# A retention, gated-FFN and four-expert kernel: low parts of the down weights by accumulating transfers, a product's operand straight from its bank, and seven products in the last unit too

## The chip, the cores and the metric

One Trainium2 chip, one of its cores. The metric is device time in microseconds of one execution; lower is better. All arithmetic on the matrix engine is fp32 split into parts: a matrix is written as high part plus low part (both in the short fp32r form), and a product of two matrices is three matrix multiplications, high by high, high by low, low by high.

## The reference

Three layers follow one another on 1536 tokens of width 512:

```python
for t in range(S):                       # B2, H8, S768, D64
    state = gamma[None, :, None, None] * state + np.einsum('bhd,bhe->bhde', k[:, :, t], v[:, :, t])
    y[:, :, t] = scale * np.einsum('bhd,bhde->bhe', q[:, :, t], state)
...
xn = x / rms * rms_g                     # DFF 1536
return (silu * val @ w_out)              # silu = g * sigmoid(g), g = xn @ w_gate, val = xn @ w_val
...
for e in range(E):                       # E 4, F 1024
    h = np.maximum(x @ w1[e], 0.0)
    out += p[:, e:e + 1] * (h @ w2[e])   # p: domain_probs over their sum
```

The change lies in the last layer, the four experts.

## The kernel before, in words

The experts' hidden columns (4 x 1024) are cut into N2 = 16 units u of 256 columns; the tokens into two halves g = 0 and 1 of 768. For each (u, g) there are an up product (512 by 256 columns of w1) and a down product (256 by 512 of w2), whose result is scaled by the expert's probability and added into `oacc[g]`.

**Up.** `winograd()` (L570) computes a 2-by-2 block product from seven products p1 to p7 instead of eight, each of 12 matmuls of 384 columns (L586). Sums of the weights' blocks (`sums`, L364) and of the tokens' blocks stand in for the blocks. PSUM banks are copied to SBUF where a product is needed twice (`kept`, L595, on ScalarE).

**Down.** `expert_out` (L1436) is plain: 6 token tiles, for each 6 matmuls of 512 columns (L1457 to L1459). `mixed_out` (L1368) takes seven products n instead, each of 9 matmuls of 256 columns (L1420), in the order n = 1, 4, 6, 5, 7, 3, 2; its weights are the two plain tiles of w2 and four differences of their quarters (`down`, made by `down_sums`, L514), its operands n the hidden blocks or sums of them (`h`, L1328). It is used for g = 0 in the units of `MIXED`, 1 to 14. Its results are added to `oacc` by VectorE (L1397): at product 7 two adds from the banks `cross`.

**Operands of the seven.** `mixed_use` (L1315) makes the operands of `mixed_out`: ReLU on ScalarE (L1339, L1346), sums by L1328, then for each operand n the high part `hs` by a ScalarE cast (L1320) and the low part `hs` by a subtraction on GpSimd or VectorE (L1322). Operand 6 is the sum made from operand 5, and that from operand 7's sum; operand 3 is made from operand 6's sum. In `expert_use`, for the units' second half, VectorE adds the kept bank (L1299), ScalarE makes the high part (L1302), VectorE the low one (L1306).

**Order on TensorE.** Within a unit: p1, p2 of (u, 0); three tiles of `expert_out` of (u-1, 1); p5, p6, p3, p7; the other three tiles; p4; then, one by one in turn, the products of (u, 1) and of `mixed_out` of (u, 0): p1, n1, p2, n4, p5, n6, p6, n5, p3, n7, p7, n3, p4, n2. One such period takes 30.6 us.

**Weights.** `piece_tasks` (L304) loads a piece of w1 or w2 (SyncE), makes its high part with ScalarE (L401) and its low part with a subtraction, `widelo` and `plainlo` (L406). `down_sums` does the same with its four differences: high part by L521, low part `downlo` by L525.

**Who does what, when.** `Pace` (L32) is a planner that runs while the program is written. A piece of work that may go to GpSimd or VectorE is added as "PV" with a level and a size, and a table of costs decides the engine and the place in its queue. Every engine then works its queue strictly in order; nothing is decided on the chip. A change of the tasks or of a cost thus moves the queues of GpSimd, VectorE and ScalarE in all later units.

Of the kernel before, what the change touches and what calls it, by code (L numbers as in the profile page):

```python
# [7 lines left out]
F32 = mybir.dt.float32  # L8
# [3 lines left out]
AF = mybir.ActivationFunctionType  # L12
ALU = mybir.AluOpType
PSUM = bass.MemoryType.PSUM

P = 128
# [146 lines left out]
def tile_retention_gated_experts(  # L163
# [27 lines left out]
    nc = tc.nc  # L191
# [8 lines left out]
    D = DM // H  # L200
# [11 lines left out]
    N2 = E * UPE  # L212
    HD = DM // 2
    MORE_HS = 2
    MIXED = set(range(1, N2 - 1))
    SEVEN = {(u, g) for u in (1,2,3,4,) for g in (1,)}
    STAGED = 3
    BIG = 3
# [85 lines left out]
    def piece_tasks(n):  # L304
# [98 lines left out]
        def low_part(eng, half):  # L403
            hi, lo = wt[key] if is_wide(key) else wt[key + (j,)]
            for t, at in parts(half):
                eng.tensor_tensor(out=at(lo), in0=t, in1=at(hi).bitcast(F32), op=ALU.subtract)  # L406

        def then(engines, size, run, *deps, gate=None, port=True):
            return pace.add(1 if key in (("g", 0), ("v", 0), ("2", 0)) else 2, engines, size, run, deps, gate, port)

# [12 lines left out]
        for half in range(2 if is_wide(key) else 1):  # L423
            size = 384 if is_wide(key) and half == 0 else NC
            last = source
            if half == 1:
                for i in range(4):
                    before = (sums_done[-2:-1] if double else sums_done[-1:]) if i == 0 else []
                    last = then("PV", P, lambda eng, i=i: sums(eng, i), last, *before)
            hi = then(  # L430
                "A", size, lambda eng, half=half: high_part(eng, half), last, *highs[-1:], gate=lambda: has_slot(key)
            )
            highs.append(hi)
            lows.append(then("PV", size, lambda eng, half=half: low_part(eng, half), hi))
        if is_wide(key):
            sums_done.append(lows[-1])
        if double:
# [58 lines left out]
    def down_sums(u, then):  # L496
# [19 lines left out]
        def high(eng, half):  # L516
# [3 lines left out]
                ]  # L520
            eng.copy(out=wt[key][0][:, 2 * half:2 * half + 2].rearrange("p n d -> p (n d)"), in_=got["t"][half])  # L521

        def low(eng, half):
            hi, lo = (w[:, 2 * half:2 * half + 2].rearrange("p n d -> p (n d)") for w in wt[key])
            eng.tensor_tensor(out=lo, in0=got["t"][half], in1=hi.bitcast(F32), op=ALU.subtract)  # L525

        gate = lambda: "T" in pools and (
            all(("S", x) in used for x, g in SEVEN) if u == min(MIXED) else u - 1 in sums_used
# [8 lines left out]
        free1 += steps[1:]  # L537
        for half in range(2):
            hi = then("A", 512, lambda eng, half=half: high(eng, half), steps[2 * half + 1], gate=gate)
            lows.append(then("PV", 512, lambda eng, half=half: low(eng, half), hi))  # L540
        tops_free.append(lows)
        ready[key] = lows

# [227 lines left out]
    def seven_out(u, g, hs):  # L771
# [7 lines left out]
        for n, half, blk in order:  # L779
# [4 lines left out]
            for j in range(KH):  # L784
# [19 lines left out]
                    [pace.done(pace.now)], port=False,  # L804
                ))
                open_chain.append(at[onto][j][-1])
            if n == 3 and g == max(x for y, x in SEVEN if y == u):
                w_used(("S", u))
            if n == 4 and g == G - 1:
                w_used(("o", u))  # L810
# [382 lines left out]
    def pair():  # L1193
        (hi, a), (lo, b) = any_tile(), any_tile()
        return hi, lo, (a, b)
# [119 lines left out]
    def mixed_use(hs):  # L1315
        h, done, read = {}, {}, {}

        def operand(n, t, dep):
# [5 lines left out]
            hs[n] = hi, lo, low, tags  # L1324
            return high, low

        def sub(out, x, y, op, *deps):
            return pace.add(0, "PV", TB, lambda eng: eng.tensor_tensor(out=out, in0=x, in1=y, op=op), deps)  # L1328

        def use(f, blk, a, b):  # L1330
# [15 lines left out]
                    0, "A", TB, lambda eng: eng.activation(out=t, in_=t, func=AF.Relu), [pace.done(end)]  # L1346
                )
            if at == (0, 0):
                read[1] = operand(1, t, done[at])
            elif at == (0, 1):  # L1350
                done[7] = sub(h[7], h[0, 0], t, ALU.subtract, done[0, 0], done[at])
                operand(7, h[7], done[7])
            elif at == (1, 1):
                operand(4, t, done[at])
                done[5] = sub(h[0, 1], h[0, 1], t, ALU.add, done[7], done[at])
                done[6] = sub(h[0, 0], h[0, 1], h[0, 0], ALU.subtract, done[5], *read[1])
                operand(5, h[0, 1], done[5])
                operand(6, h[0, 0], done[6])
            else:
                two = operand(2, t, done[at])  # L1360
                done[3] = sub(t, t, h[0, 0], ALU.subtract, done[6], *two)
                operand(3, t, done[3])
            return end
        return use

    open_sums = []

    def mixed_out(u, g, hs):  # L1368
        e = u // UPE
# [20 lines left out]
        def add(c, blk, cols, ps):  # L1390
            t = blk * CPB + c
            acc = oacc[g][:, t, cols]
            pe = p_sb[:, g * 2 * CPB + t, e:e + 1]
            if ps.shape[1] != acc.shape[1]:
                acc = acc.rearrange("p (h d) -> p h d", h=2)
                ps = ps.unsqueeze(1).to_broadcast([P, 2, HD])
            run = lambda eng: eng.scalar_tensor_tensor(out=acc, in0=ps, scalar=pe, in1=acc, op0=ALU.mult, op1=ALU.add)  # L1397
            return pace.add(1, "V", 512 if cols == every else HD + 100, run, [pace.done(pace.now)], port=False)

        plan = (  # L1400
            (1, plain_part(0, low_half), cross, lambda c: c != 1, (0, low_half, cross)),
# [7 lines left out]
        for n, moving, where, opens, result in plan:  # L1409
# [18 lines left out]
            if result:  # L1428
                blk, cols, ps = result
                for c in range(CPB):  # L1430
                    at[c].append(add(c, blk, cols, ps[c]))
                    open_sums.append(at[c][-1])
            pace.fill(3 * CPB * 0.12)
            yield

    def expert_out(u, g, hs):  # L1436
        e = u // UPE
        if u == N2 - 1:
            pace.need(*open_sums)
        w = weights(("2", u))  # L1440
        if u == 0:
            oacc.append(accp.tile([P, 2 * CPB, DM], F32, tag=f"acc{g}", name=f"oacc{g}"))
# [190 lines left out]
```

## Time and profile before

| what | value |
|---|---|
| median of 3 runs | 845.06 us (845.0 to 845.2) |
| the profiled execution, its own time | 845.45 us |
| its span, first to last instruction | 843.6 us |
| granted TensorE clock, mean | 0.998 |
| busy: TensorE, VectorE, ScalarE, GpSimd | 99%, 63%, 54%, 75% of the span |

The profile is of one execution. Around the span lie 1.85 us of its time. In the rows, PE is the matmul side of TensorE and PEld its weight loads, which overlap; DVE is VectorE, ACT ScalarE, POOL GpSimd, SP SyncE. "Idle before" an instruction, with the name of what ended it, is how a wait is read. The seven-product part of the experts begins at about 362 us, and TensorE's work ends at 839.8 us.

### The profile page before, as it was taken

The numbers are of one execution on the slowest core, as the hardware profiler recorded it, in microseconds if no ns is written. First come the engines' busy times: TensorE is split into PE (matmuls) and PEld (weight loads), VectorE is DVE, ScalarE is ACT, GpSimd is POOL, SyncE is SP. The second block draws the span as 40 slices with busy tenths as digits, with TensorE's granted clock in tenths as the row PEclk, the third lists the DMA queues.
The fourth block names the chain that finished last, engine by engine and source line by source line (L and its number), as shares of the span: only waits on it lengthen the run. The fifth ranks groups of instructions, "written<-read, shape, count | busy, mean of one in ns | idle before, by whom it ended". The sixth has DMA issues, their size and how long they took to land.

```text
span 843.6 us, 13967 instructions
## 1 busy us (share of the span) xinstructions
PE 831.1 (99%) x5143; PEld 791.8 (94%) x5143; DVE 534.6 (63%) x959; ACT 457.6 (54%) x1023; POOL 634.7 (75%) x753
## 2 busy tenths in 40 slices
PE   8989999999999999999999999999999999999998
PEld 7889999999999999889999999999999999999987
DVE  3886665877778657834565566466466556556654
ACT  4878886666665456665544544545444454454421
POOL 3457886597979676869888988988988988987500
PEclk9999999999999999999999999999999999999999
DMA  7951231232121111011011011010011011101003
GB/s 258 310 187 51 76 126 59 68 84 68 54 97 38 51 38 38 26 38 36 28 38 38 26 46 31 26 51 26 26 51 38 25 38 38 39 26 38 1 13 137
DMA packets 29232, 52.37 MB, mean 62 GB/s; under 512 B 3988, under 2 KB 12724, under 8 KB 29164
## 3 DMA queue, kind: packets, MB, share of 16 engines
q1 hardware_dynamic: 28880, 51.24, 19.3%
q8 instruction: 40, 0.66, 0.3%
q10 hardware_dynamic: 284, 0.24, 0.1%
q14 instruction: 28, 0.23, 0.1%
HBM read 48.33 MB, written 3.15 MB: 61 GB/s over the span
## 4 chain that ended last, share of the span: by engine, by line
PE 79%; DVE 7%; POOL 6%; ACT 6%; issue 2%; DMA 1%; DVEq 0%; POOLq 0%; ACTq 0%
PE bank L586 39%; PE bank L1420 7%; PE bank L1458 6%; PE bank L1459 6%; PE bank L1457 6%; PE cross L1420 5%; PE bank L797 2%; POOL widelo L406 1%; PE bank L930 1%; PE bank L1267 1%; PE bank L1268 1%; PE bank L1266 1%; PE bank L912 1%; POOL sums L364 1%; DVE sums L364 1%
## 5 line engine op out<-in xcount | busy, mean ns | idle before, releaser
L595 ACT COPY kept<-bank 128x384 f32<-128x384 f32 x150 | 71.9, 480 | 117.3 <-PE bank L586 108.0
L1397 DVE SCALAR_TENSOR_TENSOR oacc<-cross,p_sb,oacc 128x256 f32<-128x256 f32 (+1 forms) x126 | 65.6, 565 | 64.2 <-PE cross L1420 64.2
L1465 DVE SCALAR_TENSOR_TENSOR oacc<-bank,p_sb,oacc 128x512 f32<-128x512 f32 (+1 forms) x97 | 72.3, 745 | 51.9 <-PE bank L1459 51.8
L1322 POOL TENSOR_TENSOR hs<-h,hs 128x384 fp32r<-128x384 f32 x97 | 97.5, 1025 | 0.8 <-ACT hs L1320 0.8
L586 PE MATMUL bank<-x2Thi,widehi 128*128 128x384 f32 x256 | 87.7, 343 | 0.7 <-DVE kept L1299 0.7
L586 PE MATMUL bank<-x2Thi,widelo 128*128 128x384 f32 x256 | 86.2, 337 | 0.0
L586 PE MATMUL bank<-x2Tlo,widehi 128*128 128x384 f32 x256 | 85.9, 336 | 0.0
L1459 PE MATMUL bank<-plainhi,hs 128*128 128x512 f32 (+1 forms) x218 | 85.1, 390 | 0.0
L1458 PE MATMUL bank<-plainlo,hs 128*128 128x512 f32 (+1 forms) x218 | 85.0, 390 | 0.0
L1457 PE MATMUL bank<-plainhi,hs 128*128 128x512 f32 (+1 forms) x218 | 84.3, 387 | 0.0
L1302 ACT ACTIVATE hs<-kept 128x384 fp32r<-128x384 f32 x54 | 28.4, 526 | 86.9 <-DVE kept L1299 86.8
L406 POOL TENSOR_TENSOR widelo<-sums,widehi 128x512 fp32r<-128x512 f32 x49 | 63.9, 1303 | 6.5 <-ACT widehi L401 5.8
L525 POOL TENSOR_TENSOR downlo<-down,downhi 128x512 fp32r<-128x512 f32 x28 | 36.3, 1296 | 37.8 <-ACT downhi L521 37.8
L586 PE MATMUL bank<-xThi,widehi 128*128 128x384 f32 x192 | 64.5, 336 | 0.1
L586 PE MATMUL bank<-xThi,widelo 128*128 128x384 f32 x192 | 64.2, 334 | 0.0
L586 PE MATMUL bank<-xTlo,widehi 128*128 128x384 f32 x192 | 64.2, 334 | 0.0
L1397 DVE SCALAR_TENSOR_TENSOR oacc<-bank,p_sb,oacc 128x512 f32<-128x512 f32 x84 | 59.1, 744 | 6.4 <-PE bank L1420 6.3
L1328 POOL TENSOR_TENSOR h<-h 128x384 f32<-128x384 f32 x55 | 56.1, 1019 | 4.2 <-ACT h L1346 2.2
L1320 ACT CAST hs<-h 128x384 fp32r<-128x384 f32 x98 | 48.9, 513 | 16.5 <-POOL h L1328 15.2
L586 PEld LDWEIGHTS bank<-x2Thi,widehi 128*128 128x128 f32 x256 | 48.2, 188 | 4.4 <-DVE kept L1299 3.0
L1343 DVE TENSOR_TENSOR h<-bank,kept 128x384 f32<-128x384 f32 x42 | 23.3, 554 | 45.1 <-PE bank L586 44.5
L406 POOL TENSOR_TENSOR widelo<-wst,widehi 128x256 fp32r<-128x256 f32 x64 | 37.1, 601 | 17.3 <-ACT widehi L401 17.3
(240 smaller groups left out, 2689.7 us busy)
## 6 DMA issues: line engine op xcount, KB each, us to landing
wst<-in_moe_w_dram SPq DMA_DIRECT2D x64, 256.0 KB, 2.8
qk<-in_qk_dram SPq DMA_DIRECT2D x12, 512.0 KB, 5.7
wst<-in_moe_w_gate_dram SPq DMA_DIRECT2D x12, 512.0 KB, 3.8
wst<-in_moe_w_val_dram SPq DMA_DIRECT2D x12, 512.0 KB, 3.8
wst<-in_moe_w_out_dram SPq DMA_DIRECT2D x12, 512.0 KB, 3.9
vk<-in_vk_dram SPq DMA_DIRECT2D x10, 512.0 KB, 5.4
out_dram<-oacc SPq DMA_DIRECT2D x11, 256.0 KB, 2.0
vk<-in_vk_dram SPq DMA_DIRECT2D x2, 256.0 KB, 4.1
```

What stands on the lines that cost most here:

```text
L406: eng.tensor_tensor(out=at(lo), in0=t, in1=at(hi).bitcast(F32), op=ALU.subtract)
L586: nc.tensor.matmul(out=ps, lhsT=lhs, rhs=rhs, start=(first and j == i == 0), stop=(j == KH - 1 and i == 2), skip_group_check=not first,)
L595: nc.scalar.copy(out=t, in_=ps)
L1320: high = pace.add(0, "A", TB, lambda eng: eng.copy(out=hi, in_=t), [dep])
L1322: 0, "PV", TB, lambda eng: eng.tensor_tensor(out=lo, in0=t, in1=hi.bitcast(F32), op=ALU.subtract), [high]
L1328: return pace.add(0, "PV", TB, lambda eng: eng.tensor_tensor(out=out, in0=x, in1=y, op=op), deps)
L1397: run = lambda eng: eng.scalar_tensor_tensor(out=acc, in0=ps, scalar=pe, in1=acc, op0=ALU.mult, op1=ALU.add)
L1420: nc.tensor.matmul(out=where[c], lhsT=lhs[:, cols], rhs=rhs, start=bool(i == 0 and opens and opens(c)), stop=(i == 2), skip_group_check=True,)
L1457: nc.tensor.matmul(out=ps, lhsT=hi[:, c], rhs=whi[:, cols], start=(f == 0), stop=False)
L1458: nc.tensor.matmul(out=ps, lhsT=hi[:, c], rhs=wlo[:, cols], start=False, stop=False)
L1459: nc.tensor.matmul(out=ps, lhsT=lo[:, c], rhs=whi[:, cols], start=False, stop=(f == NF - 1))
L1465: nc.vector.scalar_tensor_tensor(out=acc, in0=ps, scalar=pe, in1=acc, op0=ALU.mult, op1=ALU.add)
```

## The change

`MIXED` now holds unit 15 as well, so that its g = 0 half also goes through `mixed_out`; its output tiles leave by tasks (`leaving`) after products 7 and 2. For the w2 weights of every unit in `MIXED`, the low parts are no longer subtracted: ScalarE writes the negative high part into the low tile (it copies the source with scale -1), and a transfer issued by GpSimd adds the source onto it, from DRAM for the two plain tiles, from SBUF for the two tiles of differences (four transfers of 256 KB a unit). Operand 2 takes its high and low part straight from the PSUM bank (`direct`). The planner's level of VectorE's adds from `mixed_out` goes from 1 to 0, and the weights of the SEVEN units are given back at n = 7 instead of n = 3.

```diff
--- before.py
+++ after.py
@@ -212,7 +212,7 @@
     N2 = E * UPE
     HD = DM // 2
     MORE_HS = 2
-    MIXED = set(range(1, N2 - 1))
+    MIXED = set(range(1, N2))
     SEVEN = {(u, g) for u in (1,2,3,4,) for g in (1,)}
     STAGED = 3
     BIG = 3
@@ -405,6 +405,16 @@
             for t, at in parts(half):
                 eng.tensor_tensor(out=at(lo), in0=t, in1=at(hi).bitcast(F32), op=ALU.subtract)
 
+        def negative(eng):
+            (t, at), = parts(0)
+            eng.activation(out=at(wt[key + (j,)][1]), in_=t, func=AF.Copy, scale=-1.0)
+
+        def remainder(eng):
+            (t, at), = parts(0)
+            eng.dma_start(
+                out=at(wt[key + (j,)][1]), in_=src.rearrange("p h f -> p (h f)"), accum_op=ALU.add
+            )
+
         def then(engines, size, run, *deps, gate=None, port=True):
             return pace.add(1 if key in (("g", 0), ("v", 0), ("2", 0)) else 2, engines, size, run, deps, gate, port)
 
@@ -431,7 +441,11 @@
                 "A", size, lambda eng, half=half: high_part(eng, half), last, *highs[-1:], gate=lambda: has_slot(key)
             )
             highs.append(hi)
-            lows.append(then("PV", size, lambda eng, half=half: low_part(eng, half), hi))
+            if key[0] == "2" and key[1] in MIXED:
+                minus = then("A", size, negative, hi)
+                lows.append(then("P", 200, remainder, minus, port=False))
+            else:
+                lows.append(then("PV", size, lambda eng, half=half: low_part(eng, half), hi))
         if is_wide(key):
             sums_done.append(lows[-1])
         if double:
@@ -520,9 +534,15 @@
                 ]
             eng.copy(out=wt[key][0][:, 2 * half:2 * half + 2].rearrange("p n d -> p (n d)"), in_=got["t"][half])
 
+        def negative(eng, half):
+            eng.activation(
+                out=wt[key][1][:, 2 * half:2 * half + 2].rearrange("p n d -> p (n d)"), in_=got["t"][half],
+                func=AF.Copy, scale=-1.0,
+            )
+
         def low(eng, half):
-            hi, lo = (w[:, 2 * half:2 * half + 2].rearrange("p n d -> p (n d)") for w in wt[key])
-            eng.tensor_tensor(out=lo, in0=got["t"][half], in1=hi.bitcast(F32), op=ALU.subtract)
+            lo = wt[key][1][:, 2 * half:2 * half + 2].rearrange("p n d -> p (n d)")
+            eng.dma_start(out=lo, in_=got["t"][half], accum_op=ALU.add)
 
         gate = lambda: "T" in pools and (
             all(("S", x) in used for x, g in SEVEN) if u == min(MIXED) else u - 1 in sums_used
@@ -537,7 +557,8 @@
         free1 += steps[1:]
         for half in range(2):
             hi = then("A", 512, lambda eng, half=half: high(eng, half), steps[2 * half + 1], gate=gate)
-            lows.append(then("PV", 512, lambda eng, half=half: low(eng, half), hi))
+            hi = then("A", 512, lambda eng, half=half: negative(eng, half), hi)
+            lows.append(then("P", 200, lambda eng, half=half: low(eng, half), hi, port=False))
         tops_free.append(lows)
         ready[key] = lows
 
@@ -804,7 +825,7 @@
                     [pace.done(pace.now)], port=False,
                 ))
                 open_chain.append(at[onto][j][-1])
-            if n == 3 and g == max(x for y, x in SEVEN if y == u):
+            if n == 7 and g == max(x for y, x in SEVEN if y == u):
                 w_used(("S", u))
             if n == 4 and g == G - 1:
                 w_used(("o", u))
@@ -1324,6 +1345,15 @@
             hs[n] = hi, lo, low, tags
             return high, low
 
+        def direct(n, ps):
+            hi, lo, tags = pair()
+            nc.scalar.activation(out=hi, in_=ps, func=AF.Relu)
+            end = pace.did("A", TB)
+            nc.vector.scalar_tensor_tensor(
+                out=lo, in0=ps, scalar=0.0, in1=hi.bitcast(F32), op0=ALU.max, op1=ALU.subtract
+            )
+            hs[n] = hi, lo, pace.done(pace.did("V", TB, end)), tags
+
         def sub(out, x, y, op, *deps):
             return pace.add(0, "PV", TB, lambda eng: eng.tensor_tensor(out=out, in0=x, in1=y, op=op), deps)
 
@@ -1346,7 +1376,11 @@
                     0, "A", TB, lambda eng: eng.activation(out=t, in_=t, func=AF.Relu), [pace.done(end)]
                 )
             if at == (0, 0):
-                read[1] = operand(1, t, done[at])
+                if b is None:
+                    direct(1, a)
+                    read[1] = ()
+                else:
+                    read[1] = operand(1, t, done[at])
             elif at == (0, 1):
                 done[7] = sub(h[7], h[0, 0], t, ALU.subtract, done[0, 0], done[at])
                 operand(7, h[7], done[7])
@@ -1357,13 +1391,13 @@
                 operand(5, h[0, 1], done[5])
                 operand(6, h[0, 0], done[6])
             else:
-                two = operand(2, t, done[at])
-                done[3] = sub(t, t, h[0, 0], ALU.subtract, done[6], *two)
+                direct(2, a)
+                done[3] = sub(t, t, h[0, 0], ALU.subtract, done[6], done[at])
                 operand(3, t, done[3])
             return end
         return use
 
-    open_sums = []
+    open_sums, leaving = [], []
 
     def mixed_out(u, g, hs):
         e = u // UPE
@@ -1395,7 +1429,7 @@
                 acc = acc.rearrange("p (h d) -> p h d", h=2)
                 ps = ps.unsqueeze(1).to_broadcast([P, 2, HD])
             run = lambda eng: eng.scalar_tensor_tensor(out=acc, in0=ps, scalar=pe, in1=acc, op0=ALU.mult, op1=ALU.add)
-            return pace.add(1, "V", 512 if cols == every else HD + 100, run, [pace.done(pace.now)], port=False)
+            return pace.add(0, "V", 512 if cols == every else HD + 100, run, [pace.done(pace.now)], port=False)
 
         plan = (
             (1, plain_part(0, low_half), cross, lambda c: c != 1, (0, low_half, cross)),
@@ -1430,13 +1464,17 @@
                 for c in range(CPB):
                     at[c].append(add(c, blk, cols, ps[c]))
                     open_sums.append(at[c][-1])
+                    if u == N2 - 1 and n in (7, 2):
+                        t = blk * CPB + c
+                        acc, to = oacc[g][:, t, :], out[(g * 2 * CPB + t) * P:(g * 2 * CPB + t + 1) * P, :]
+                        leaving.append(pace.add(1, "D", 0, lambda eng, acc=acc, to=to: eng.dma_start(out=to, in_=acc), [at[c][-1]]))
             pace.fill(3 * CPB * 0.12)
             yield
 
     def expert_out(u, g, hs):
         e = u // UPE
         if u == N2 - 1:
-            pace.need(*open_sums)
+            pace.need(*open_sums, *leaving)
         w = weights(("2", u))
         if u == 0:
             oacc.append(accp.tile([P, 2 * CPB, DM], F32, tag=f"acc{g}", name=f"oacc{g}"))
```

`direct(1, a)` never runs: at (0, 0) the second argument is always given in these units.

In numbers of instructions: TensorE keeps its order but for the last unit, where 36 matmuls of 512 columns become 63 of 256. GpSimd goes from 758 to 626 instructions, 60 of them the new transfers; it gives up 58 low parts of w2, 24 low parts of operands and about 110 sums and low parts of w1, most of these two kinds to VectorE, which goes from 961 to 1115. ScalarE goes from 1018 to 1087 (60 negatives and 14 ReLUs from the bank more). SyncE's queue is the same. Up to 362 us all queues are the same.

The queue of GpSimd (POOL) in a middle unit, from the last differences of the down weights to operand 3. First before; `hs_7683`, `7673`, `7685`, `7687`, `7738`, `7740` are the low parts of operands 4, 7, 5, 6, 2, 3:

```order
L514 TENSOR_TENSOR down_7661<-wst_7636,wst_7533 128x256
L514 TENSOR_TENSOR down_7661<-wst_7636,down_7660 128x256
L1328 TENSOR_TENSOR h_7669<-h_7598,h_7670 128x384
L1322 TENSOR_TENSOR hs_7683<-h_7669,hs_7682 128x384
L1328 TENSOR_TENSOR h_7670<-h_7670,h_7669 128x384
L1328 TENSOR_TENSOR h_7598<-h_7670,h_7598 128x384
L1322 TENSOR_TENSOR hs_7673<-h_7669,hs_7672 128x384
L1322 TENSOR_TENSOR hs_7685<-h_7670,hs_7684 128x384
L1322 TENSOR_TENSOR hs_7687<-h_7598,hs_7686 128x384
L1322 TENSOR_TENSOR hs_7738<-h_7735,hs_7737 128x384
L1328 TENSOR_TENSOR h_7735<-h_7735,h_7598 128x384
L406 TENSOR_TENSOR widelo1_7585<-sums_7626,widehi1_7584 128x4x128
```

And the same stretch with the change, in units 2 to 13 alike; `hs_8424`, `8411`, `8426`, `8428` are the low parts of operands 4, 7, 5, 6:

```order
L406 TENSOR_TENSOR widelo1_8337<-sums_8366,widehi1_8336 128x4x128
L528 TENSOR_TENSOR down_8413<-wst_8250 128x256
L528 TENSOR_TENSOR down_8413<-wst_8388,down_8413 128x256
L1358 TENSOR_TENSOR h_8407<-h_8330,h_8408 128x384
L528 TENSOR_TENSOR down_8414<-wst_8388,wst_8250 128x256
L1343 TENSOR_TENSOR hs_8424<-h_8407,hs_8423 128x384
L364 TENSOR_TENSOR sums_8455<-wst_8439 128x128
L1343 TENSOR_TENSOR hs_8411<-h_8407,hs_8410 128x384
L1358 TENSOR_TENSOR h_8408<-h_8408,h_8407 128x384
L1358 TENSOR_TENSOR h_8330<-h_8408,h_8330 128x384
L1358 TENSOR_TENSOR h_8476<-h_8476,h_8330 128x384
L1343 TENSOR_TENSOR hs_8426<-h_8408,hs_8425 128x384
```

The row that follows is `hs_8428`, operand 6. The low part `widelo` of w1's sums (128x4x128) and the sum of operand 3 (`h_8476`), which stood behind operand 6's low part, now stand ahead of it, with one `sums`; the low part of operand 2 is gone from this queue.

The same queue in unit 14 with the change, where the transfers of the last unit's plain low parts come into it:

```order
L1343 TENSOR_TENSOR hs_9124<-h_9107,hs_9123 128x384
L1343 TENSOR_TENSOR hs_9111<-h_9107,hs_9110 128x384
L528 TENSOR_TENSOR down_9114<-wst_9088,down_9113 128x256
L414 DMA plainlo0_9163<-in_moe2_w2_dram 128x512
L1358 TENSOR_TENSOR h_9108<-h_9108,h_9107 128x384
L1358 TENSOR_TENSOR h_9030<-h_9108,h_9030 128x384
L414 DMA plainlo1_9194<-in_moe2_w2_dram 128x512
L1358 TENSOR_TENSOR h_9173<-h_9173,h_9030 128x384
L1343 TENSOR_TENSOR hs_9128<-h_9030,hs_9127 128x384
L1343 TENSOR_TENSOR hs_9180<-h_9173,hs_9179 128x384
```

Here two transfers stand between operand 7's low part (`hs_9111`) and operand 6's (`hs_9128`); operand 5's low part is VectorE's.

The queue of VectorE (DVE) around product 7's adds in a middle unit, before; `kept_8147` is the sum that frees the bank of p4:

```order
L1299 TENSOR_TENSOR kept_8170<-bank_8140,kept_8170 128x384
L1397 SCALAR_TENSOR_TENSOR oacc0_4346<-bank_8104,p_sb_81,oacc0_4346 128x512
L1397 SCALAR_TENSOR_TENSOR oacc0_4346<-cross_8100,p_sb_81,oacc0_4346 128x512 x2
L1299 TENSOR_TENSOR kept_8147<-bank_8088,kept_8147 128x384
L1306 SCALAR_TENSOR_TENSOR hs_8126<-kept_8096,hs_8125 128x384
L1306 SCALAR_TENSOR_TENSOR hs_8194<-kept_8170,hs_8193 128x384
```

and with the change, where `kept_8899` is that sum:

```order
L1320 TENSOR_TENSOR kept_8923<-bank_8892,kept_8923 128x384
L1431 SCALAR_TENSOR_TENSOR oacc0_4344<-bank_8852,p_sb_81,oacc0_4344 128x512
L1327 SCALAR_TENSOR_TENSOR hs_8948<-kept_8923,hs_8947 128x384
L1431 SCALAR_TENSOR_TENSOR oacc0_4344<-cross_8848,p_sb_81,oacc0_4344 128x512
L1320 TENSOR_TENSOR kept_8899<-bank_8836,kept_8899 128x384
L1431 SCALAR_TENSOR_TENSOR oacc0_4344<-cross_8848,p_sb_81,oacc0_4344 128x512
```

One low part and one add from `cross` stand between the last add from a bank and the sum, where two adds stood; the low part of p2's block (`hs_8875<-kept_8844`, not shown) also moves to the middle of the unit.

## Rows read from the trace of the kernel before

**Rows 1.** The page, part 1: busy time, share of the span, instructions, by engine.

```profile
PE 831.1 (99%) x5143; PEld 791.8 (94%) x5143; DVE 534.6 (63%) x959; ACT 457.6 (54%) x1023; POOL 634.7 (75%) x753
```

**Rows 2.** Windows, one period: length, busy PE, PEld, DVE, ACT, POOL; clock, DMA share, GB/s.

```profile
739.43:770.02 30.59, 30.59 (x185) 28.93 (x184) 18.18 (x32) 14.37 (x32) 26.89 (x33) 1.00 0.12 35
```

**Rows 3.** Waits: engine, line <- releaser: us in all, times, longest.

```profile
PEld bank L586 <- DVE kept L1299: 3.0, 13, 1.0
```

**Rows 4.** Timeline of POOL, same period: start, us, engine, line, operation, [idle before].

```profile
743.96 1.29 POOL L406 TENSOR_TENSOR widelo<-sums,widehi 128x512 fp32r<-128x512 f32 x1
745.21 1.02 POOL L1322 TENSOR_TENSOR hs<-h,hs 128x384 fp32r<-128x384 f32 x1
...
748.55 0.46 POOL L364 TENSOR_TENSOR sums<-wst,sums 128x128 f32<-128x128 f32 x1
748.97 0.74 POOL L514 TENSOR_TENSOR down<-wst 128x256 f32<-128x256 f32 x1
749.78 0.74 POOL L514 TENSOR_TENSOR down<-wst,down 128x256 f32<-128x256 f32 x1
750.48 0.74 POOL L514 TENSOR_TENSOR down<-wst 128x256 f32<-128x256 f32 x1
...
751.89 1.01 POOL L1328 TENSOR_TENSOR h<-h 128x384 f32<-128x384 f32 x1
752.86 1.02 POOL L1322 TENSOR_TENSOR hs<-h,hs 128x384 fp32r<-128x384 f32 x1
753.83 2.12 POOL L1328 TENSOR_TENSOR h<-h 128x384 f32<-128x384 f32 x2
755.90 3.94 POOL L1322 TENSOR_TENSOR hs<-h,hs 128x384 fp32r<-128x384 f32 x4
```

**Rows 5.** Timeline of ACT, same period.

```profile
747.94 0.48 ACT L595 COPY kept<-bank 128x384 f32<-128x384 f32 x1 [0.56 <-PE bank L586]
...
750.08 0.61 ACT L401 CAST widehi<-sums 128x512 fp32r<-128x512 f32 x1
```

**Rows 6.** Timeline of TensorE, same period: product n = 6 and what follows it.

```profile
760.28 0.28 PE L1420 MATMUL cross<-downhi,hs 128*128 128x256 f32 x1
...
760.40 0.30 PEld L1420 LDWEIGHTS cross<-downhi,hs 128*128 128x128 f32 x2
...
761.34 0.34 PE L586 MATMUL bank<-x2Thi,widehi 128*128 128x384 f32 x1
```

**Rows 7.** Timeline of all engines, same period: from product 7's adds to p4.

```profile
765.89 1.40 DVE L1397 SCALAR_TENSOR_TENSOR oacc<-cross,p_sb,oacc 128x512 f32<-128x512 f32 x2
...
767.21 0.54 DVE L1299 TENSOR_TENSOR kept<-bank,kept 128x384 f32<-128x384 f32 x1
...
767.56 0.28 PE L1420 MATMUL bank<-plainhi,hs 128*128 128x256 f32 x1
767.67 1.02 DVE L1306 SCALAR_TENSOR_TENSOR hs<-kept,hs 128x384 fp32r<-128x384 f32 x2
767.81 0.19 PEld L586 LDWEIGHTS bank<-x2Thi,widehi 128*128 128x128 f32 x1 [0.17 <-DVE kept L1299]
```

**Rows 8.** The costliest groups: POOL's low parts of operands, all 97.

```profile
L1322 POOL TENSOR_TENSOR hs<-h,hs 128x384 fp32r<-128x384 f32 x97 | 97.5, 1025 | 0.8 <-ACT hs L1320 0.8
```

**Rows 9.** DMA issues: what, queue, count, KB each, median us to landing; timeline of SP.

```profile
wst<-in_moe_w_dram SPq DMA_DIRECT2D x64, 256.0 KB, 2.8
...
773.36 0.34 SPq L316 DMA_DIRECT2D wst<-in_moe_w_dram  x1
```

**Rows 10.** Timeline of PE, last unit: three tiles of the plain down product of g = 0.

```profile
802.58 0.39 PE L1457 MATMUL bank<-plainhi,hs 128*128 128x512 f32 x1
...
806.71 0.33 PE L586 MATMUL bank<-x2Thi,widehi 128*128 128x384 f32 x1
```

**Rows 11.** Timeline of DVE and POOL, the period after: two low parts at once.

```profile
782.67 0.57 DVE L1322 TENSOR_TENSOR hs<-h,hs 128x384 fp32r<-128x384 f32 x1
...
782.79 1.33 POOL L1322 TENSOR_TENSOR hs<-h,hs 128x384 fp32r<-128x384 f32 x1
```

## The prediction

> **What bounds the kernel now.** I read the shares of the page first [rows 1]: TensorE is busy 99% of the span, the next engine, GpSimd, 75%. So the sum of TensorE's work is the time, and a change pays only by taking matmuls away or by ending a wait of TensorE; it costs whatever new wait it makes. Then the window of one period of the expert part [rows 2]: of 30.59 us TensorE works 30.59, while GpSimd works 26.89 and VectorE 18.18. The reader should see that GpSimd is close to full yet makes nobody wait. Taking 58 subtractions from GpSimd relieves an engine that is not waited for. Third, the list of waits: in the expert part TensorE has one wait that repeats, 13 times for 3.0 us in all, for VectorE's sum that frees the bank of p4 [rows 3]. That is what there is to win. Last the timelines, to see how much slack the operands of the seven down products have, since the order on TensorE stays the same but the queues of its feeders do not.
>
> **Low parts by transfers.** Removed from GpSimd: 58 subtractions. They stood beside matmuls, and nobody waited. Added on ScalarE: 60 negatives of about 0.6 us (the cast of as many elements takes 0.61 [rows 5]), 2.4 us per period on an engine that works 14.4 of 30.6 [rows 2]; nothing, so long as they stand behind the urgent ones, and if that cover goes ScalarE's kept copy comes up to 0.6 late. Added on GpSimd: 60 issues, of price D. The trace of before has no transfer issued by GpSimd. Bounds: 0.34 us, an issue on SyncE's queue, and 2.8 us, a 256 KB transfer from issue to landing [rows 9]. I take 1.0, near their geometric middle, since the issue is nearer to what an engine's queue is held for than the landing. The Trainium skill, "DMA: Bandwidth & Descriptors", Specifications, gives about 1 us to the first byte of a transfer issued by GpSimd; by that estimate the sum would be the same. In the units 2 to 13 the four issues stand where GpSimd has nothing urgent behind them: two after operand 3's low part, two at the unit's start. Landing is used 15 us later or more. The removed subtractions were 1.3 us each, so GpSimd has room. Cost there 0. The transfers' traffic, 1 MB a period on queues that are 12% busy, costs 0 too.
>
> **The moved chain: operand 6.** This is the main term. Before, GpSimd went from the differences through h7, operand 4, h5, h6 and operands 7, 5, 6; the third of the four low parts that start at 755.90 is operand 6's [rows 4], so it ended at 755.90 + 2 x 0.97 + 1.02 = 758.86. TensorE loads the weights of the first matmul that reads it at 760.40, just after product 6 begins at 760.28 [rows 6]: 1.5 us of slack. With the change `widelo` stands ahead of this chain, and it cannot start before ScalarE has cast the sums' high part, which now stands behind ScalarE's copy of p6. That copy starts at 747.94, released by TensorE, and takes 0.48; the cast takes 0.61 [rows 5]: 749.03. From there, start to start by the rows of [rows 4]: widelo 1.25 (743.96 to 745.21), two differences 0.81 + 0.70, h7 0.97, a difference 0.70, operand 4 0.97, a `sums` 0.42, operand 7 0.97, h5 and h6 2.07, the sum of operand 3 1.04 (half of that pair), operand 5 0.97, operand 6 1.02 to its end. Sum 11.89, so it ends at 760.92, and with 0.06 until the reader starts (in [rows 7] the sum ends at 767.75, the load it releases starts at 767.81) at 760.98. Needed at 760.40: TensorE stands 0.58 us. The chain is anchored to TensorE within each unit, so the wait does not melt away in later units: 12 units alike, 2 to 13, 12 x 0.58 = **+7.0**. The ends: 0.3 us (the steps of the chain at their fastest, 0.02 each lower) and 0.9 (a step or two beside a VectorE subtraction), 3.6 to 10.8. Behind the waiting matmuls stand all of TensorE's; nothing overtakes. Operands 5, 7 and 3 are needed later than they come.
>
> In unit 1 the chain is shorter and in unit 15 VectorE has part of it: 0. In unit 14 two issues of transfers come between operand 7 and operand 6, while operand 5 is VectorE's, there is no `sums`, and one difference more stands ahead: 11.89 - 0.97 - 0.42 + 0.70 = 11.20, and 2 D. From 749.03 to 760.40, less the 0.06, there are 11.31: about 2 D - 0.1 late, **+1.9** at D = 1.0, 0.6 to 5.5 between the bounds.
>
> **Product 7's adds and p4.** Before, two adds from `cross`, 1.40 us as a pair, precede the sum that frees p4's bank; the sum starts at 767.21, ends at 767.75, and TensorE's last matmul of n = 3 started at 767.56, with the next one due 0.12 later at 767.68. It started at 767.81 [rows 7]: 0.13 lost. With the change one add (0.66, half the start-to-start of the pair) and one low part (about 0.47 start to start, from the 1.02 for two) stand ahead: 0.19 earlier, so the wait goes. 12 x 0.13 = **-1.6** (0 to -3.0, all of [rows 3]). What is late next there is nothing: the bank's readers are done.
>
> **Operand 2 from the bank.** Its high part becomes a ReLU in place of a cast, on ScalarE both; its low part goes from GpSimd to VectorE, which is idle a third of the period; operand 2 is read last of all: 0. The weights freed at n = 7 instead of n = 3, and the level of the adds: they move queue places that are counted above, 0 by themselves.
>
> **The last unit.** 18 matmuls of 512 take 802.58 to 806.71 = 4.13 us [rows 10], so 36 take 8.26. Nine matmuls of a seven-product take 760.28 to 761.34 = 1.06 [rows 6], seven of them 7.42. **-0.8**. The adds behind it are 128x256 and 128x512 pieces on VectorE, beside matmuls of p1 to p7 of the other half; the output transfers leave before the end. The end itself, the last plain tile with its add and transfer, is the same.
>
> **Sum**, on the profiled execution: 845.45 + 7.0 + 1.9 - 1.6 - 0.8 = 851.95. It stood 0.4 over the median of the runs shown: **851.6**.
>
> **Rivals.**
> *A, the forecast*: 851.6, on its own 847 to 856.
> *B, the two low parts collide.* VectorE's low part of p2's block moves to the middle of the unit, beside GpSimd's operands 5 and 6, if ScalarE's high part for it comes early. When such a pair ran at once before, GpSimd's subtraction took 1.33 us instead of 1.025 [rows 11, 8]. That would be 0.31 a unit more: 12 x 0.31 = 3.7, so 855.3. Against: I find VectorE's to be ready some 0.2 us after GpSimd's last has begun. The Trainium skill, "SBUF — State Buffer", Who interferes with whom, says that a VectorE instruction with two SBUF inputs and a GpSimd one that reads SBUF lock each other out whole, the second waiting for the first. The trace agrees in kind but not in full: GpSimd started 0.12 after VectorE's 0.57 us and lost 0.31 instead of 0.45.
> *C, on the other side: operand 6 comes in time.* The wait vanishes if the chain is 0.58 us, 5% of its 11.9, shorter, or its start that much earlier (a cast that ScalarE does before its copy, say); from 11.3 us downward nothing is lost. Then 845.45 + 0.6 to 1.9 - 1.6 - 0.8 = 843.65 to 844.95, less 0.4: 843.3 to 844.6. For it: the chain is put together from single rows. Against: the 97 low parts of operands on GpSimd have a mean of 1025 ns [rows 8], so the steps hardly vary.
> *D, the issue is dear.* With D at 2.8 unit 14 loses 5.5 instead of 1.9, 855.2; and GpSimd's differences, pushed later, then run beside VectorE's low parts, up to the 3.7 of B more: 858.9. Against: an issue need not last until the landing.
> *E, the last unit's saving is not there*, as its operands come late to TensorE: 0.8 more, inside A's range.
>
> **How the numbers follow.** A 0.60 with E, B 0.15, D 0.08, C 0.17. What a measurement of this kernel can tell from no change is about 0.2%, 1.7 us: below 843.4 is faster, above 846.8 slower. C lies about 843.4 and above, 0.09 faster (with a shorter issue or more won at p4) and 0.08 same; 0.03 of A ends within 0.2%. Faster 0.09, same 0.11, slower 0.80. The range leaves out the lower half of C and the upper part of D: 844.0 to 858.0; the slower cases alone have 847 to 858.
>
> **What would show it.** Right: among the waits of TensorE a new group at the matmuls of `cross` (n = 6) released by GpSimd's low part `hs`, 12 or 13 times, about 0.6 us each, a period of 31.0 to 31.1 us, and one longer in unit 14. The 13 waits on VectorE's kept sum are gone or down to a few. GpSimd's busy time falls by over 100 us with an idle stretch ahead of `widelo` in each period: a relieved engine, and a later one. The last unit's g = 0 shows 63 matmuls of 256. B shows as low parts on GpSimd of 1.3 us where operand 6's stands, D as a wait in unit 14 of over 3 us. Wrong would be a period of 30.4 to 30.6 with no wait at n = 6 (then C), or a wait of TensorE on a weight's low part, whose transfer would have landed late.

## The result and the profile after

| | median | lowest to highest |
|---|---|---|
| before, beside it | 845.03 us | 844.69 to 845.20 |
| the change | 851.43 us | 851.29 to 852.02 |
| a second run of both: before | 844.31 us | 843.98 to 844.57 |
| the change | 851.32 us | 851.02 to 851.62 |

Ratio 1.0076 (95% interval 1.0058 to 1.0095), in the second run 1.0082 (1.0067 to 1.0098): slower by some 0.8%. The forecast was 851.6 us, with a wait of 0.58 us at product 6 in twelve units. The first part of the profile's page, the busy time of each engine, against [rows 1]:

```profile
PE 831.5 (98%) x5170; PEld 792.5 (93%) x5170; DVE 598.7 (70%) x1113; ACT 490.7 (58%) x1092; POOL 531.7 (63%) x621
```

GpSimd was relieved of 103 us, and the kernel got slower. The list of TensorE's waits, against [rows 3]:

```profile
PEld cross L1454 <- POOL hs L1343: 8.3, 13, 1.5
...
PEld bank L607 <- DVE kept L1320: 1.0, 1, 1.0
```

The 12 waits of 0.17 us before p4 are gone (a single one of 1.0, ahead of 360 us, is in both kernels); 13 new ones stand at product 6. GpSimd's timeline in the period of unit 13, which answers to [rows 4]:

```profile
753.69 1.29 POOL L406 TENSOR_TENSOR widelo<-sums,widehi 128x512 fp32r<-128x512 f32 x1 [5.23 <-ACT widehi L401]
754.95 0.74 POOL L528 TENSOR_TENSOR down<-wst 128x256 f32<-128x256 f32 x1
755.76 0.75 POOL L528 TENSOR_TENSOR down<-wst,down 128x256 f32<-128x256 f32 x1
756.46 1.01 POOL L1358 TENSOR_TENSOR h<-h 128x384 f32<-128x384 f32 x1
757.43 0.74 POOL L528 TENSOR_TENSOR down<-wst 128x256 f32<-128x256 f32 x1
758.13 1.02 POOL L1343 TENSOR_TENSOR hs<-h,hs 128x384 fp32r<-128x384 f32 x1
759.11 0.46 POOL L364 TENSOR_TENSOR sums<-wst 128x128 f32<-128x128 f32 x1
759.53 1.01 POOL L1343 TENSOR_TENSOR hs<-h,hs 128x384 fp32r<-128x384 f32 x1
760.51 3.19 POOL L1358 TENSOR_TENSOR h<-h 128x384 f32<-128x384 f32 x3
763.66 1.98 POOL L1343 TENSOR_TENSOR hs<-h,hs 128x384 fp32r<-128x384 f32 x2
```

Read it from the bracket: GpSimd stands idle 5.23 us, its queue held by `widelo`, which waits for ScalarE's cast. Then it works without a gap to the end of operand 6's low part, 763.66 + 1.98 = 765.64: 11.95 us for what this text calls the chain. TensorE and VectorE at that place, against [rows 6]:

```profile
764.71 1.35 DVE L1327 SCALAR_TENSOR_TENSOR hs<-kept,hs 128x384 fp32r<-128x384 f32 x1 [1.05 <-ACT hs L1323]
...
764.94 0.28 PE L1454 MATMUL cross<-downhi,hs 128*128 128x256 f32 x1
...
765.70 0.30 PEld L1454 LDWEIGHTS cross<-downhi,hs 128*128 128x128 f32 x2 [0.56 <-POOL hs L1343]
...
766.63 0.34 PE L607 MATMUL bank<-x2Thi,widehi 128*128 128x384 f32 x1
```

Product 6 runs from 764.94 to 766.63, 1.69 us where it took 1.06: TensorE loses 0.63, of which the row of the load shows 0.56. Unit 14's load at 797.70 has 1.50, its product 6 takes 2.62. The period, against [rows 2], now 31.07:

```profile
743.86:774.93 31.07, 30.71 (x186) 29.00 (x185) 22.43 (x43) 16.33 (x36) 18.51 (x22) 1.00 0.33 68
```

GpSimd works 18.5 of 31.07 us and is nevertheless what TensorE waits for.

### The profile page after: what moved, and what is told of

It reads as the page before. It is cut to its first block, busy times and chain, and to the rows that moved or that the text cites. A ratio compares the mean times of both kernels' runs of the same rounds, so it can differ in the third digit from the quotient of the medians.

```text
span 849.7 us, 14142 instructions
## 1 busy us (share of the span) xinstructions
PE 831.5 (98%) x5170; PEld 792.5 (93%) x5170; DVE 598.7 (70%) x1113; ACT 490.7 (58%) x1092; POOL 531.7 (63%) x621
## 4 chain that ended last, share of the span: by engine, by line
PE 47%; POOL 22%; issue 15%; ACT 8%; DVE 7%; DMA 1%; POOLq 0%; SPq 0%; ACTq 0%; DVEq 0%
PE bank L607 24%; PE bank L1454 6%; POOL hs L1343 6%; POOL h L1358 5%; PE cross L1454 4%; POOL down L528 3%; POOL widelo L406 2%; POOL sums L364 2%; PE bank L818 2%; POOL downlo L545 1%; PE bank L1496 1%; PE bank L1497 1%; PE bank L1495 1%; PE bank L1288 1%; PE bank L951 1%
## 5 line engine op out<-in xcount | busy, mean ns | idle before, releaser
L406 POOL TENSOR_TENSOR widelo<-sums,widehi 128x512 fp32r<-128x512 f32 x36 | 46.8, 1300 | 74.7 <-ACT widehi L401 73.9
L1503 DVE SCALAR_TENSOR_TENSOR oacc<-bank,p_sb,oacc 128x512 f32<-128x512 f32 (+1 forms) x91 | 67.6, 744 | 36.6 <-PE bank L1497 36.5
L545 POOL DMA_DIRECT2D downlo<-down x30 | 26.4, 879 | 105.1 <-ACT downlo L538 85.1
L1343 POOL TENSOR_TENSOR hs<-h,hs 128x384 fp32r<-128x384 f32 x73 | 74.4, 1032 | 9.8 <-issue 9.2
L1497 PE MATMUL bank<-plainhi,hs 128*128 128x512 f32 (+1 forms) x206 | 80.4, 390 | 0.0
L1496 PE MATMUL bank<-plainlo,hs 128*128 128x512 f32 (+1 forms) x206 | 80.3, 390 | 0.0
L1495 PE MATMUL bank<-plainhi,hs 128*128 128x512 f32 (+1 forms) x206 | 79.7, 387 | 0.0
L1431 DVE SCALAR_TENSOR_TENSOR oacc<-cross,p_sb,oacc 128x256 f32<-128x256 f32 (+1 forms) x135 | 70.2, 567 | 12.3 <-PE cross L1454 12.3
L1431 DVE SCALAR_TENSOR_TENSOR oacc<-bank,p_sb,oacc 128x512 f32<-128x512 f32 x90 | 63.2, 745 | 6.8 <-PE bank L1454 6.8
L1327 DVE SCALAR_TENSOR_TENSOR hs<-kept,hs 128x384 fp32r<-128x384 f32 x51 | 41.8, 821 | 14.3 <-ACT hs L1323 14.3
L607 PEld LDWEIGHTS bank<-x2Tlo,widehi 128*128 128x128 f32 x256 | 48.2, 188 | 1.3
```

The lines of the kernel that those rows point to most:

```text
L607: nc.tensor.matmul(out=ps, lhsT=lhs, rhs=rhs, start=(first and j == i == 0), stop=(j == KH - 1 and i == 2), skip_group_check=not first,)
L1343: 0, "PV", TB, lambda eng: eng.tensor_tensor(out=lo, in0=t, in1=hi.bitcast(F32), op=ALU.subtract), [high]
L1495: nc.tensor.matmul(out=ps, lhsT=hi[:, c], rhs=whi[:, cols], start=(f == 0), stop=False)
L1496: nc.tensor.matmul(out=ps, lhsT=hi[:, c], rhs=wlo[:, cols], start=False, stop=False)
L1497: nc.tensor.matmul(out=ps, lhsT=lo[:, c], rhs=whi[:, cols], start=False, stop=(f == NF - 1))
L1503: nc.vector.scalar_tensor_tensor(out=acc, in0=ps, scalar=pe, in1=acc, op0=ALU.mult, op1=ALU.add)
```

## The experiments

Ratios are to the kernel before, run beside each on the same chip (its medians there 844.3 to 844.4). Where two experiments are compared in microseconds, they can come from two chips.

**1. Operand 6 first.**

```diff
-                operand(5, h[0, 1], done[5])
-                operand(6, h[0, 0], done[6])
+                six = operand(6, h[0, 0], done[6])
+                operand(5, h[0, 1], six[0])
```

> All transfers, negatives, the bank operand and the last unit stay; operand 5's cast is made to wait for operand 6's, which moves operand 6's low part from GpSimd's queue to VectorE's, behind the sum for p2. Theory (TensorE loses its time only to operand 6's low part coming late in GpSimd's order): the twelve waits of 0.56 us go, 6.7 us, and of unit 14's 1.5 at least 1.0: 851.4 - 7.7 to 8.2 = 843.2 to 843.7 us, no group of waits of the cross matmuls on a low part. Rival (the transfers or their traffic slow the chain or the matmuls): the time stays above 847 us, with waits elsewhere or longer matmuls.

842.18 us, ratio 0.9974 (0.9965 to 0.9984): 2.2 us below the kernel before, somewhat more than the 1.3 to 1.8 that the expectation comes to against 845.0. No wait at product 6 is left but one of 0.36 us in unit 1, and the period is 30.42. So the late operand 6 is more than the whole loss; without it the change gains. (This edit also moves other work between GpSimd and VectorE; experiment 5 moves nothing else.)

**2. The same order without the transfers.** `negative` stays, the two `dma_start` with `accum_op` are left out.

> The sixty accumulating transfers are not issued, so the low parts of the mixed units' w2 weights are left as the negative high parts; every other instruction stands in the same order. Theory: the queue order is what costs, so the twelve waits of 0.56 us stay; only unit 14's wait of 1.5 us goes, since two issues of 0.88 us leave its chain: 851.4 - 1.5 = 849.9 us. Rival (issue, traffic or landing of the transfers delays the matmuls): the time falls to 844 to 845 us and the waits on operand 6 vanish.

849.88 us, ratio 1.0068 (1.0052 to 1.0083), 5.5 us above before. The waits, 12 of 0.56 to 0.59 us, and one of 0.20 in unit 14 where the change has 1.50:

```profile
765.85 0.30 PEld L1454 LDWEIGHTS cross<-downhi,hs 128*128 128x128 f32 x2 [0.56 <-POOL hs L1343]
...
796.55 0.30 PEld L1454 LDWEIGHTS cross<-downhi,hs 128*128 128x128 f32 x2 [0.20 <-POOL hs L1343]
```

The waits of the twelve middle units don't come from issue, traffic or landing of the transfers. What is left is the order in which the rest of GpSimd's work stands, which experiment 5 tests; only unit 14's wait is mostly the two issues. The expectation had none left there. The 0.20 is a collision:

```profile
794.79 0.83 DVE L1343 TENSOR_TENSOR hs<-h,hs 128x384 fp32r<-128x384 f32 x1
...
795.17 1.33 POOL L1343 TENSOR_TENSOR hs<-h,hs 128x384 fp32r<-128x384 f32 x1
```

Operand 6's low part begins 0.38 us behind a low part of VectorE's and takes 1.33 us in place of 1.02. In the change that part of VectorE's is over before operand 6's begins.

**3. Operand 2 made as before**, and **4. the transfers alone** on the kernel before.

```diff
-                direct(2, a)
-                done[3] = sub(t, t, h[0, 0], ALU.subtract, done[6], done[at])
+                two = operand(2, t, done[at])
+                done[3] = sub(t, t, h[0, 0], ALU.subtract, done[6], *two)
```

Experiment 4 has this too, with `MIXED` to unit 14, the adds' level 1 and `n == 3`.

> Operand 2 is made as in the kernel before (cast, then a low part on GpSimd), the rest of the change stays. Theory: in the chain ahead of operand 6 the low part of operand 2 (0.97 us) takes the place of the sum of operand 3 (1.04), so the wait is 0.5 us and stays in all twelve units: 850.5 to 851.0 us, and unit 14 as the planner makes it. Rival (taking operand 2 from the bank caused the late operand 6): the wait goes and the time is 844 to 845 us.

> Only the low parts by transfers, on the kernel before: operand 2 as before, the last unit plain, the level of the adds 1, the weights freed at n = 3. Theory: the freed time on GpSimd lets the planner put widelo ahead of the chain, so the wait of about 0.5 us a unit appears with this part alone, 12 to 13 times 0.5, and the p4 waits (1.6 to 2.0 us) are gone with it: 845.0 + 6.0 to 6.5 - 1.6 to 2.0 = 849.0 to 849.9 us. Rival (the wait needs the other parts of the change): 843 to 845 us.

853.87 us, ratio 1.0115 (1.0101 to 1.0128), and 853.43 us, 1.0108 (1.0094 to 1.0122). The waits are there in both, so the transfers alone, with the negatives that belong to them, bring them. But they are 0.77 us in nearly all units, not 0.5, and both times lie some 3 us above what was expected. Experiment 3's timeline shows why:

```profile
764.78 3.26 POOL L1343 TENSOR_TENSOR hs<-h,hs 128x384 fp32r<-128x384 f32 x3
...
766.44 0.74 DVE L1327 SCALAR_TENSOR_TENSOR hs<-kept,hs 128x384 fp32r<-128x384 f32 x1 [0.59 <-ACT hs L1323]
...
768.09 0.30 PEld L1454 LDWEIGHTS cross<-downhi,hs 128*128 128x128 f32 x2 [0.77 <-POOL hs L1343]
```

Three low parts take 3.26 us, where three at 0.97 from start to start and 1.02 for the last make 2.96. VectorE's low part of p2 begins at 766.44, GpSimd's third (operand 6) after two steps of 0.97 at 766.72: second by 0.28 us, and it pays 0.3. Experiment 4 has the same rows. That is the collision of rival B, in two neighbouring kernels. My expectations had left it out.

**5. Only the places of operands 5 and 6 exchanged** in GpSimd's queue, in the units where both are there, with no other instruction moved.

```diff
+        if getattr(task, "behind", None) is not None and task.behind.end is None and engine == "P":
+            task.behind.then = lambda: task.run(self.engines[engine])
+        else:
+            task.run(self.engines[engine])
+        getattr(task, "then", lambda: None)()
...
+                five = operand(5, h[0, 1], done[5])
+                five[1].behind = operand(6, h[0, 0], done[6])[1]
```

> All of the change stays; the only difference is that in GpSimd's queue the low part of operand 6 stands ahead of that of operand 5, in the units where both are there (no other queue moves, the planner's clocks are the same). Theory (place in the queue): operand 6 is ready 0.97 us earlier against a wait of 0.56, so the twelve waits go, and 12 times the 0.63 us that TensorE loses at product 6 with them; unit 14's stays, as its operand 5 is VectorE's. 7.5 us below the changed kernel, about 1.1 us below the kernel before: ratio 0.9985 to 0.9990. Rival (the freed p4 waits and the last unit give nothing, and the change's cost is spread over ports and traffic): over 1.003.

844.03 us, ratio 0.9991 (0.9977 to 1.0004). One wait is left, unit 14's:

```profile
790.02 0.30 PEld L1458 LDWEIGHTS cross<-downhi,hs 128*128 128x128 f32 x2 [1.50 <-POOL hs L1347]
```

Two instructions of one queue exchanged give back 7.3 us (851.32 to 844.03), where 7.5 was expected. Against the kernel before, 0.9985 to 0.9990 was expected; the ratio by itself can't be told from no change.

**6. Experiment 1 without transfers**, the low parts by subtraction.

```diff
-            if key[0] == "2" and key[1] in MIXED:
+            if False:
...
-            eng.dma_start(out=lo, in_=got["t"][half], accum_op=ALU.add)
+            eng.tensor_tensor(
+                out=lo, in0=got["t"][half],
+                in1=wt[key][0][:, 2 * half:2 * half + 2].rearrange("p n d -> p (n d)").bitcast(F32), op=ALU.subtract)
...
-            hi = then("A", 512, lambda eng, half=half: negative(eng, half), hi)
-            lows.append(then("P", 200, lambda eng, half=half: low(eng, half), hi, port=False))
+            lows.append(then("PV", 512, lambda eng, half=half: low(eng, half), hi))
```

> The first experiment's kernel (operand 5's cast behind operand 6's) with the low parts of w2 and its differences made by subtraction as in the kernel before; operand 2 from the bank and the seven products in the last unit stay. Theory: TensorE is the bound and the 58 subtractions are waited for by nobody, so the transfers give nothing by themselves; as VectorE's queue here has the one add and one low part ahead of the sum that frees p4's bank, the gain is that of the first experiment, ratio 0.997 to 0.9985. Rival (the transfers' relief of GpSimd is what the first experiment gained): ratio 0.9995 or more, with waits on GpSimd.

841.04 us, ratio 0.9961 (0.9949 to 0.9974), no wait of TensorE from 360 us on. That is below the 0.997 to 0.9985 expected. The transfers gave experiment 1 nothing; this one is even some 1.1 us faster in the medians and 0.8 in the profiled executions. Of these 0.8, 0.4 lie at the wait of unit 1 and 0.3 behind product 6 of unit 15; what makes the latter stays open.

**7. The last unit alone**, on the kernel before: `MIXED` to unit 15 and the `leaving` tasks.

> The kernel before with one part of the change alone: the last unit's first half also by seven products. Theory: 36 matmuls of 512 against 63 of 256, 8.26 against 7.42 us, so 0.8 us less, ratio 0.9990; the p4 waits of 0.17 stay. Rival (operands of the last unit come late, or its adds lengthen the end): 0 to 2 us more.

843.26 us, ratio 0.9988 (0.9979 to 0.9997): 1.05 us less. All 12 waits of 0.17 us before p4 are still there.

**8. The change with the last unit plain**, `MIXED` to unit 14.

> The change without the seven products in the last unit. Theory: 0.8 us more for the matmuls, 1.56 less because unit 14's transfers for the last unit leave the chain, the twelve waits of 0.56 stay: 0.8 us below the changed kernel, 5.6 us above the kernel before, ratio 1.0066. Rival: unit 14 waits all the same, ratio 1.0085.

850.80 us, ratio 1.0078 (1.0063 to 1.0094), 0.5 us below the change's 851.32: of the sign expected, but no difference that these runs can tell. The trace shows the parts: twelve waits of 0.56 to 0.58 and none in unit 14.

**9. The whole change but for the transfers**, in the change's own order of operands 5 and 6 (experiment 6's edit on the changed kernel), beside **10. the change again**.

> The whole change but for the transfers: the low parts of w2 and of its differences are subtractions again, the order of operands 5 and 6 is the change's own. Theory (the transfers free GpSimd, the planner fills it with widelo ahead of the chain, and operand 6 comes late): with the subtractions back, widelo stands behind operand 6's low part again, the chain is that of before with operand 3's sum in it, 1.04 later, 759.9 against 760.34, so there is no wait at product 6; the p4 waits are gone, the last unit saves its 0.8 to 1.05: ratio 0.996 to 0.9975. Rival (the bank operand and the last unit have their share of the late operand 6): waits of 0.2 us or more a unit, ratio 0.999 or more.

> The changed kernel as it is, on the same chip as the run beside it, to have both on one footing: ratio 1.0076 to the kernel before, twelve waits of 0.56 us and one of 1.5.

841.14 us, ratio 0.9963 (0.9951 to 0.9976), beside the change's 851.32. GpSimd's busy time:

```profile
PE 828.1 (99%) x5170; PEld 791.9 (94%) x5170; DVE 570.2 (68%) x1024; ACT 460.2 (55%) x1032; POOL 610.0 (73%) x710
```

With 610 us of work on GpSimd instead of 532 the kernel is 10.2 us faster and has no wait at product 6 in any unit. In the units 2, 4 and so on to 14 the order is the one expected: `widelo` stands behind operand 6's low part. Unit 12, where product 6 begins at 726.75:

```profile
723.38 1.03 POOL L1357 TENSOR_TENSOR h<-h 128x384 f32<-128x384 f32 x1
724.35 2.97 POOL L1342 TENSOR_TENSOR hs<-h,hs 128x384 fp32r<-128x384 f32 x3
727.27 1.30 POOL L406 TENSOR_TENSOR widelo<-sums,widehi 128x512 fp32r<-128x512 f32 x1
```

In the odd units from 3 to 13 the planner made another chain, in which VectorE has one of the sums and two of the low parts; there is no wait there either. Experiments 6 and 9 beat both kernels.

## Why the prediction was right

**The wait of operand 6** was forecast at 0.58 us in 12 units, +7.0. Its own steps: `widelo` starts 1.09 us after ScalarE's copy of p6 began; measured 1.08 (752.61 to 753.69):

```profile
752.61 0.48 ACT L616 COPY kept<-bank 128x384 f32<-128x384 f32 x1 [0.56 <-PE bank L607]
752.98 0.62 ACT L401 CAST widehi<-sums 128x512 fp32r<-128x512 f32 x1
```

The cast stood behind that copy before the change, too (750.08 in [rows 5]), and ScalarE waits 0.56 us ahead of the copy: it is `widelo` that moved, and the negatives don't hold the cast up. The chain was forecast at 11.89; measured 11.95. The wait was forecast at 0.58; the load shows 0.56, and the matmuls of product 6 lose 0.63. Against the period of 30.42 that experiments 1, 6 and 9 reach, without a wait at product 6 or at p4, the period of 31.07 holds 0.65: 12 times that are 7.8 instead of 7.0. Experiment 5 shows that it is the place in the queue.

**Unit 14** was forecast at +1.9 with D = 1.0. In the page's DMA issues the transfers from SBUF hold the queue 0.879 us on the mean, those from DRAM 1.021. In unit 14 there are 12.88 us from the chain's start at 784.76 to 797.64, 0.06 ahead of the load that waits; less the 11.20 of the forecast this leaves 0.84 for each. (Experiment 2 gives back only 1.30 for both, since operand 6 pays 0.31 for its collision there.) The period there is 32.05 against 30.37 in experiment 6: 1.7.

**The wait of p4** was forecast at -1.6, as 0.13 a unit. The period before, 30.60 on the mean, less 30.42 is 0.18, so -2.2: the term was too small, since I took what the last matmul's spacing showed, and the wait's own row had 0.17 [rows 7]. That the wait goes with the order of VectorE's queue is seen in all ten runs: in experiment 7, which keeps the order, it stays, in the others it is gone.

**The last unit** was forecast at -0.8; its seven products take 1.06 us each in the trace as forecast, 7.42 us. Experiment 7 measured -1.05, with an interval that holds both.

**Sum**: 7.8 + 1.7 - 2.2 - 1.05 = +6.3, where I had +6.5; measured 6.4 and 7.0 in the medians, 6.1 in the spans. Two errors, 0.8 too little for the wait and about as much too little for the gains (0.6 at p4, 0.25 in the last unit), cancel. That the 851.6 lies so near to 851.43 is luck; the terms themselves are off by 0.2 to 0.8.

**The rivals.** C, operand 6 in time, fell. D, the dear issue, fell: 0.84 instead of 2.8. B happened in part: in the twelve middle units, here unit 13, VectorE's low part began at 764.71, forecast some 0.2 us after GpSimd's last had begun, measured 0.07 after (763.66 + 0.98 = 764.64). So GpSimd was first, and VectorE paid: 1.35 us in place of the 0.56 that it takes on the mean in the kernel before. Experiment 3 shows the other case; its period is 31.30, 0.23 us more than the change's. The Trainium skill, "SBUF — State Buffer", Who interferes with whom, has it that the one that begins first keeps the other out; the trace of these units agrees on who pays, and on the size nearly: a whole lockout would have made VectorE's 0.93 + 0.56 = 1.49 us, measured 1.35. Unit 14, in the last section, does not follow it.

**What no term said** is the larger half of the lesson: the change's other parts are worth 3.2 us, and the transfers took that and 7 more. I had costed the transfers at nothing but unit 14 and put the wait down to a moved chain; experiments 4 and 9 show the link. That `widelo` stands ahead of the chain with the transfers (experiment 4) and not without them (experiment 9) is shown. Why the planner puts it there is not: I read it as the room that 58 subtractions leave on GpSimd, and the 5.23 us that `widelo` waits for its cast as time that the planner's clocks don't have, but no run takes these subtractions away without adding the 60 negatives on ScalarE.

## What to carry to other kernels

Relief of an engine that nobody waits for was worth nothing by itself here, and with a planner that orders the queues anew it cost: look for what now stands ahead of the instruction that the bound engine reads next. To price such a change, take one period, find the anchor (the last release by the bound engine), add the rows of the queue from there to the reader, and compare with when it is needed; here 0.6 us in a chain of 12 decided whether twelve units lose 7 us or nothing. When a moved queue is the suspect, exchange two of its instructions and nothing else.

## What the runs showed of the hardware

An accumulating transfer of 256 KB, issued by GpSimd, holds its queue about as long as a subtraction of 128x384 (0.88 and 1.02 us on the mean against 1.02), and from issue to landing it takes longer than SyncE's plain ones of that size (2.8 us):

```profile
plainlo<-in_moe_w_dram POOLq DMA_DIRECT2D x30, 256.0 KB, 4.4
downlo<-down POOLq DMA_DIRECT2D x30, 256.0 KB, 3.5
```

No instruction waits for these landings in the trace. The instruction behind an issue starts before the issue's row ends, and is itself longer: in unit 14

```profile
791.83 0.85 POOL L414 DMA_DIRECT2D plainlo<-in_moe_w_dram  x1
792.46 2.38 POOL L1358 TENSOR_TENSOR h<-h 128x384 f32<-128x384 f32 x2
794.78 0.89 POOL L414 DMA_DIRECT2D plainlo<-in_moe_w_dram  x1
795.39 1.32 POOL L1358 TENSOR_TENSOR h<-h 128x384 f32<-128x384 f32 x1
...
795.84 3.20 DVE L1327 SCALAR_TENSOR_TENSOR hs<-kept,hs 128x384 fp32r<-128x384 f32 x1 [0.59 <-ACT hs L1323]
...
796.37 2.25 POOL L1343 TENSOR_TENSOR hs<-h,hs 128x384 fp32r<-128x384 f32 x2
```

the two sums take 2.38 us where two took 2.12 [rows 4], the third 1.32 where one took 1.01; 0.84 is the price with this overlap taken in.

Of two colliding low parts, in the middle units of these kernels, the one that began second paid: VectorE 0.07 us behind lost 0.8, GpSimd 0.28 behind lost 0.3. The last rows above show that this is not the whole rule. VectorE's low part begins 0.45 us behind a sum of GpSimd's and 0.53 ahead of the first of two low parts, operand 6's; it takes 3.20 us where its mean before was 0.56, and ends at 799.04, behind both (798.62). GpSimd's three instructions begin 0.98 and 0.96 us apart, as they do undisturbed (0.97). What decides here who goes first, no run shows.
